# Residual input by accumulating DMA transfers, six kept sums and another split of token blocks, in a spectral filter plus MLP kernel

## The chip, the cores and the metric

The kernel runs on one core of one Trainium2 chip. The metric is the device time of one execution in microseconds (us). Eleven runs of the kernel before gave a median of 158.83 us. The engines of the core are TensorE (PE in the profile; PEld is its weight load), VectorE (DVE), ScalarE (ACT), GpSimd (POOL) and SyncE (SP, which here only issues transfers).

## What is computed

```python
def reference(A_x, A_w_r, A_w_i, B_x, B_w1, B_b1, B_w2, B_b2):
    def _A_ref(x, w_r, w_i):
        B, S, D = x.shape                       # 1, 2048, 640
        X = rfft2(x.astype(jnp.float32), axes=(-2, -1))
        X = X * (w_r + 1j * w_i)
        return irfft2(X, s=(S, D), axes=(-2, -1)).astype(jnp.bfloat16)
    def _B_ref(x, w1, b1, w2, b2):              # w1 640x1536, w2 1536x640
        h = jnp.einsum("bsd,df->bsf", x, w1) + b1
        h = _gelu(h)
        return jnp.einsum("bsf,fd->bsd", h, w2) + b2
    x = A_x
    xn = _layernorm(x, axis=-1)
    return x + _A_ref(xn, A_w_r, A_w_i) + _B_ref(xn, B_w1, B_b1, B_w2, B_b2)
```

All inputs are bf16. The output is the sum of three terms: the residual input `x`, a filter in the two-dimensional frequency domain, and an MLP with GELU. Both branches read the same normalised input.

## The kernel before

**Chunks.** The 2048 tokens are 16 chunks of 128 partitions x 640. Each chunk is loaded into `XV`, its statistics are taken (L575, L577), the reciprocal root is a power on GpSimd (L583), and the chunk is normalised (L594). For chunks 0 to 5 the transpose that the MLP needs is made on TensorE (L603); for chunks 6 to 15 by transposing transfers that SyncE issues (L614). The result is `xnT`. SyncE issues them in between the loads of the filter weights, each of which waits until the one five places earlier has landed.

**MLP, first half.** `BLOCKS` splits the chunks into seven token blocks, before: (0), (1), (2,3), (4,5), (6,7,8), (9,10,11), (12 to 15). For each block and each of 12 slices of the hidden size, five matmuls of the block's width (128, 256, 384 or 512 columns) fill a PSUM tile `hps`, and ScalarE writes `gT` from it with bias and GELU (L661). `ZONE` says which of the eight PSUM banks a tile may take, `PRIO` the rank of each kind of work.

**Spectral branch.** Both transforms are matmuls with cosine and sine tables. Forward, along tokens and features: folding adds on VectorE (L626, L630), then `gtab` matmuls into `XW`, `etab` matmuls into `Xb`, `mtab` matmuls into `Y`, for eight pairs of frequencies. The filter is L717 (products) and L722 (`Z`); small gathers `Zs` follow (L487, L488, and L485 on ScalarE). Back: `ntab` matmuls into `XV`, `getab` matmuls (one group for every two chunks) into `yo`, unfolding adds L810 (`y2`) and L815 (`yf`), and `htab` matmuls that add the last transform onto the chunk's PSUM tile.

**MLP, second half, and output.** For most chunks 24 matmuls `W`,`gT` of 320 columns and then two `htab` matmuls fill one PSUM tile `fps`. For the chunks in `STAGED` (0, 2, 4, 7, 9) the 24 matmuls are done early, while the spectral branch is in progress, and VectorE adds the bias `b2` and keeps the sum in fp32 in `xnT`, which is no longer needed by then (L796); their `htab` matmuls fill a tile of their own later. Every output chunk needs a tile `xo` of what is to be added to PSUM: SyncE loads the residual chunk into `xr` (L826), GpSimd adds it to the kept sum, or to the bias, in fp32 (L827), VectorE adds PSUM and this tile into `ost` (L840), and SyncE stores `ost` (L842). `xr` has four buffers, `xo` three and `ost` three.

**Order.** A planner (`Sched`) takes operations with an engine, a guessed duration, a priority and what they read and write, and lays down one fixed order for each engine; the time at which it ends a transfer is a guess too. A wait is put in where an operation needs another engine's or a transfer's result. The engines then run their lists in order, so an instruction that waits holds all that stands behind it on its engine. `gate` orders two operations in the plan without a wait; `after` gives a wait. Of the GpSimd adds, chunk 0's waits for the last `Z`; those of chunks 1 to 5 wait for the output add of chunk 0, and each later one for the output add five places earlier (`PACE = 5`), all by this line:

```python
port=True, reads=[xr, B_b2b] + ([B_st2[c]] if c in STAGED else []), writes=[xo], after=[z_last] + os_ops[max(c - PACE, 0):][:1])
```

The line numbers of the changed kernel lie one lower than these from the buffers' lines on, up to the output loop, where L827 becomes L826 (the bias copy) and L828 (the transfer), and L840 stays.

Of the kernel before, what the change touches and what calls it, by code (L numbers as in the profile page):

```python
# [8 lines left out]
F32 = dt.float32  # L9
# [4 lines left out]
D = 640  # L14
# [96 lines left out]
def pool_us(n):  # L111
    return 0.075 + n / 500.0


ZONE = {'hps': ((2, 8), (0, 8), (5, 8), (4, 8), (4, 8), (4, 8), (4, 8)), 'bps': (0, 4), 'cps': (0, 8), 'dps': (0, 4), 'eps': (0, 4), 'fps': (4, 8), 'fst': (4, 8), 'yps': (0, 8), 'tps': (0, 2), 'aps': (0, 6)}
PRIO = {'hps': 40.1, 'gelu': 176.7, 'pb': 71.8, 'pc': 120.9, 'filt': 194.1, 'ipc': 347.6, 'xb': 272.1, 'eps': 47.7, 'fin': 1, 'fst': 11.8}
BLOCKS = ((0, 1), (1, 2), (2, 4), (4, 6), (6, 9), (9, 12), (12, 16))
AHEAD = 2
STAGED = (0, 2, 4, 7, 9)
XRAT = 4  # L120
LAG = 5
# [63 lines left out]
class Sched:  # L185
# [10 lines left out]
    def op(self, engs, prio, emit, reads=(), writes=(), after=(), nbytes=0, gate=(), rate=360e3, bias=BIAS, port=False):  # L196
        o = Op()
        o.name = writes[0].name if writes else ""
        o.engs, o.prio, o.emit = engs, prio, emit
        o.reads, o.writes, o.after, o.gate = list(reads), list(writes), list(after), list(gate)  # L200
        o.nbytes, o.rate, o.bias, o.port = nbytes, rate, bias, port
        o.seq = len(self.ops)
        o.eng, o.done, o.inc, o.count, o.sem = None, False, False, None, None
        o.deps = [w for b in o.reads for w in b.writers] + list(after)
        for b in o.reads:
            b.readers.append(o)
        for b in o.writes:
            b.writers.append(o)
        self.ops.append(o)
        return o  # L210

    def schedule(self):
# [23 lines left out]
        while left:  # L236
# [45 lines left out]
            if o.nbytes:  # L282
                s = max(t + 1.2, dma_free)
                dma_free = s + o.nbytes / o.rate
                o.end = dma_free + (1.8 if o.seq > FAST else 0.6)
            else:
                o.end = t + dur + LAT[e]
# [105 lines left out]
def bass_parallel_sum__spectral_gfnet__dense_activation_gelu__prompt_kernel(  # L393
# [21 lines left out]
    with ExitStack() as es:  # L415
        def sb(name, shape, dtype=BF):
            return es.enter_context(nc.sbuf_tensor(name, shape, dtype))
# [33 lines left out]
        xrt = sb("xr", [128, 4, D])  # L451
        xot = sb("xo", [128, 3, D], F32)
# [17 lines left out]
        p_yo, p_y2, p_yf, p_xr, p_xo, p_os = Pool(3), Pool(2), Pool(3), Pool(4), Pool(3), Pool(3)  # L470

        def load(dst, src, buf, nbytes, after=(), reads=(), rate=330e3, eng="sp"):
            return K.op([(eng, 0.45)], 0, lambda e, _: e.dma_start(dst, src), reads=reads, writes=[buf], after=after, nbytes=nbytes, rate=rate)  # L473
# [56 lines left out]
        def load_w(dst, src, nbytes, rate):  # L530
            few.append(load(dst, src, B_w, nbytes, after=few[-DEPTH:][:1] if len(few) >= DEPTH else [], rate=rate))
# [53 lines left out]
        for c in range(16):  # L585
# [27 lines left out]
            else:  # L613
                ring_ops.append(K.op([("sp", 1.25)], 50, lambda e, _, c=c, xnv=xnv: e.dma_start(  # L614
                    xnT[:, :, 128 * c:128 * c + 128], xnv(0, [[1, D]]), transpose=True), reads=[xn], writes=[B_xnT[c]], nbytes=163840, rate=200e3))
# [33 lines left out]
        for blk, (c0, c1) in enumerate(BLOCKS):  # L649
            s0, s1 = 128 * c0, 128 * c1  # L650
            for fc in range(NFC):
                hps = Buf(f"hps{blk}_{fc}", psum, 1, ZONE["hps"][blk])
# [138 lines left out]
        def halves(v):  # L791
            return v.rearrange("p (h n) -> p h n", n=H2)
        for i, c in enumerate(STAGED):
            fps, B_st2[c] = Buf(f"fst{c}", psum, 2, ZONE["fst"]), Buf(f"sum{c}")
            st_ops += second(c, (0, 1), fps, all_hps, True)
            K.op([("dve", dve_us(D))], 86, lambda e, _, i=i, fps=fps: e.tensor_tensor(  # L796
                out=halves(xnT[:, i, 0:2 * D].bitcast(F32)), in0=ps2(fps.slot, H2), in1=halves(b2bc[:]), op=ALU.add), reads=[fps, B_b2b], writes=[B_st2[c]], after=all_hps)
        for cp in range(8):
# [20 lines left out]
            for n in range(2):  # L819
                c = 2 * cp + n  # L820
                xr, xo = Buf(f"xr{c}", p_xr), Buf(f"xo{c}", None if c in STAGED else p_xo)

                def xov(a, b, c=c, xo=xo):

                    return halves(xnT[:, STAGED.index(c), 2 * a:2 * b].bitcast(F32) if c in STAGED else xot[:, xo.slot, a:b])
                K.op([("sp", 0.35)], 0, lambda e, _, c=c, xr=xr: e.dma_start(xrt[:, xr.slot, :], xv[:, c, :]), writes=[xr], nbytes=163840, gate=pb_ops[XRAT:XRAT + 1])  # L826
                K.op([("pool", pool_us(640))], 50, lambda e, _, c=c, xr=xr, xov=xov: e.tensor_tensor(  # L827
                    out=xov(0, D), in0=halves(xrt[:, xr.slot, :]), in1=xov(0, D) if c in STAGED else halves(b2bc[:]), op=ALU.add),  # L828
                    port=True, reads=[xr, B_b2b] + ([B_st2[c]] if c in STAGED else []), writes=[xo], after=[z_last] + os_ops[max(c - PACE, 0):][:1])
                part = []  # L830
                for hs in ((0, 1),) if c < 15 else ((0,), (1,)):
                    os_, fps = Buf(f"os{c}_{hs[0]}", p_os), Buf(f"fps{c}_{hs[0]}", psum, 2, ZONE["yps" if c in STAGED else "fps"])
                    a, b = H2 * hs[0], H2 * (hs[-1] + 1)
                    if c not in STAGED:
# [6 lines left out]
                        out=halves(ost[:, os_.slot, a:b]), in0=ps2(fps.slot, H2)[:, hs[0]:hs[-1] + 1, :], in1=xov(a, b), op=ALU.add), reads=[fps, xo], writes=[os_]))  # L841
# [33 lines left out]
```

## Time and profile before

| what | value |
|---|---|
| median of 11 runs | 158.83 us (158.0 to 161.4) |
| the profiled execution | 159.16 us |
| its span in the profile | 157.4 us |
| TensorE busy | 148.1 us, 94% |
| VectorE busy | 124.8 us, 79% |
| ScalarE busy | 80.0 us, 51% |
| GpSimd busy | 31.0 us, 20% |
| granted TensorE clock | 0.998 of full speed |

The profiled execution's own time is 1.76 us above its span and 0.33 us above the median. "Busy" is the time in which an engine had an instruction in work; matmuls overlap, so two that follow each other closely count as one busy stretch. In the rows of the order of time, the first number is the start in us, the second the length, "x" the number of instructions that were merged, and the brackets hold the idle time before them with the instruction that seems to have ended it. In the table by stretch, each engine's column is its busy time, with its number of instructions. In the groups, what follows the bar is the total busy time in us and the mean of one in ns. In the list of transfers the numbers are the size in KB and the median us from issue to landing.

### The profile page before, as it was taken

How to read it: one execution, taken by the hardware profiler on the slowest of the kernel's cores; microseconds unless marked ns; L12 is line 12 of the kernel's file. 1: busy time of each engine (PE TensorE's matmuls, PEld its weight loads, DVE VectorE, ACT ScalarE, POOL GpSimd, SP SyncE). 2: the span in 40 equal slices, each digit the busy share in tenths (PEclk: the TensorE clock that was granted, in tenths of full speed). 3: DMA queues.
4: the chain of work that ended last, by engine and by line, in shares of the span. 5: the costliest groups of instructions: out<-in, count | busy, mean ns of one | idle time of the engine just before them, and what ended most of it. 6: DMA issues, size and time to landing. Idle time of an engine off the chain costs nothing.

```text
span 157.4 us, 3731 instructions
## 1 busy us (share of the span) xinstructions
PE 148.1 (94%) x1528; PEld 99.9 (63%) x1533; DVE 124.8 (79%) x263; ACT 80.0 (51%) x168; POOL 31.0 (20%) x33
## 2 busy tenths in 40 slices
PE   5799999979999999999999999899999799999993
PEld 2399799845566554445457666566776466777771
DVE  3759999979994697699498699787999999992231
ACT  3189889957777779789776456323101103100000
POOL 1201112210200000000000000300999652344200
PEclk9999999999999999999999999999999999999999
DMA  4999926979899000218513000100264433211121
GB/s 106 334 361 399 248 80 139 227 175 88 166 180 243 6 0 0 76 53 254 167 12 119 0 4 0 40 5 0 83 191 146 140 110 131 83 42 42 54 75 42
DMA packets 20648, 18.19 MB, mean 116 GB/s; under 512 B 8088, under 2 KB 19352, under 8 KB 20504
## 3 DMA queue, kind: packets, MB, share of 16 engines
q1 hardware_dynamic: 20464, 17.92, 42.4%
q8 instruction: 12, 0.20, 0.6%
q10 hardware_dynamic: 168, 0.04, 0.1%
q14 instruction: 4, 0.03, 0.1%
HBM read 13.69 MB, written 2.62 MB: 104 GB/s over the span
## 4 chain that ended last, share of the span: by engine, by line
PE 67%; DVE 12%; DMA 7%; ACT 4%; SPq 3%; POOL 3%; issue 3%; DVEq 0%; ACTq 0%
PE ps L478 66%; DMA XV<-in_A_x_dram 5%; DVE Wf L815 3%; SPq L473 3%; DMA out_dram<-ost 2%; POOL xo L827 2%; DVE ost L840 2%; ACT Xb L485 2%; DVE stats L575 1%; POOL xnT L827 1%; DVE Wf L810 1%; DVE T L717 1%; DVE xnT L796 1%; DVE Zs L488 1%; ACT Wf L485 1%
## 5 line engine op out<-in xcount | busy, mean ns | idle before, releaser
L478 PE MATMUL ps<-xnT,W 128*128 128x128 bf16 (+3 forms) x415 | 56.3, 287 | 3.0 <-ACT gT L661 1.0
L478 PE MATMUL ps<-W,gT 128*128 128x320 bf16 x384 | 56.6, 299 | 0.0
L478 PEld LDWEIGHTS ps<-W,gT 128*128 128x128 bf16 x384 | 36.7, 98 | 14.7 <-issue 0.8
L661 ACT ACTIVATE gT<-ps,b1col 128x128 bf16<-128x128 f32 (+3 forms) x84 | 39.8, 507 | 10.7 <-PE ps L478 9.7
L478 PEld LDWEIGHTS ps<-xnT,W 128*128 128x128 bf16 x420 | 34.0, 98 | 17.6 <-ACT gT L661 3.2
L827 POOL TENSOR_TENSOR xo<-xr,b2bc 128x640 f32<-128x640 bf16 x11 | 16.6, 1512 | 21.7 <-DVE ost L840 21.7
L485 ACT ACTIVATE Wf<-ps 128x640 bf16<-128x640 f32 x10 | 6.8, 703 | 25.2 <-PE ps L478 25.2
L827 POOL TENSOR_TENSOR xnT<-xr,xnT 128x640 f32<-128x640 bf16 x5 | 7.8, 1563 | 59.4 <-DVE Z L722 57.9
L840 DVE TENSOR_TENSOR ost<-ps,xo 128x640 bf16<-128x640 f32 (+1 forms) x12 | 9.1, 762 | 10.4 <-PE ps L478 10.3
L575 DVE BATCH_NORM_STATS2 stats<-XV 128x6 f32<-128x320 bf16 x32 | 14.1, 472 | 2.7 <-DMA XV<-in_A_x_dram 2.6
L815 DVE TENSOR_TENSOR Wf<-Wf 128x640 bf16<-128x640 bf16 x16 | 13.8, 893 | 0.1
L717 DVE TENSOR_TENSOR T<-Y,Wf 128x1288 bf16<-128x1288 bf16 x16 | 12.6, 828 | 0.9 <-ACT Y L485 0.4
L583 POOL TENSOR_TENSOR rstd<-ve,mhalf 128x2 f32<-128x2 f32 (+1 forms) x9 | 6.5, 720 | 33.8 <-DVE ve L582 33.8
L485 ACT ACTIVATE XV<-ps 128x640 bf16<-128x640 f32 x11 | 7.4, 703 | 5.9 <-PE ps L478 5.8
L810 DVE TENSOR_TENSOR Wf<-Wf 128x640 bf16<-128x640 bf16 x16 | 9.7, 642 | 0.8 <-ACT Wf L485 0.8
L488 DVE CAST Y<-ps 128x644 bf16<-128x644 f32 x8 | 6.6, 828 | 4.5 <-PE ps L478 4.5
L478 PE MATMUL ps<-getab,XV 128*128 128x160 bf16 (+1 forms) x128 | 8.6, 233 | 0.9 <-DVE ost L840 0.9
L485 ACT ACTIVATE Xb<-ps 128x640 bf16<-128x640 f32 x9 | 7.9, 894 | 2.7 <-PE ps L478 2.7
L478 PE MATMUL ps<-etab,XW 128*128 128x160 bf16 (+1 forms) x128 | 8.6, 233 | 0.0
L478 PEld LDWEIGHTS ps<-getab,XV 128*128 128x128 bf16 (+1 forms) x128 | 5.3, 95 | 4.3 <-DVE ost L840 1.5
L488 DVE CAST Xb<-ps 128x640 bf16<-128x640 f32 x7 | 6.2, 885 | 2.0 <-PE ps L478 2.0
L485 ACT ACTIVATE XW<-ps 128x640 bf16<-128x640 f32 x11 | 7.5, 702 | 0.6 <-PE ps L478 0.4
(51 smaller groups left out, 136.7 us busy)
## 6 DMA issues: line engine op xcount, KB each, us to landing
W<-in_B_w_dram SPq DMA_DIRECT2D x8, 480.0 KB, 4.9
xr<-in_A_x_dram SPq DMA_DIRECT2D x16, 160.0 KB, 2.3
out_dram<-ost SPq DMA_DIRECT2D x15, 160.0 KB, 1.8
XV<-in_A_x_dram SPq DMA_DIRECT2D x7, 320.0 KB, 8.1
Wf<-in_A_w_r_dram SPq DMA_DIRECT2D x7, 160.5 KB, 5.2
Wf<-in_A_w_i_dram SPq DMA_DIRECT2D x7, 160.5 KB, 3.7
gtab<-c_G SPq DMA_DIRECT2D x1, 512.0 KB, 7.4
htab<-c_H SPq DMA_DIRECT2D x1, 512.0 KB, 5.1
```

The lines of the kernel that those rows point to most:

```text
L473: return K.op([(eng, 0.45)], 0, lambda e, _: e.dma_start(dst, src), reads=reads, writes=[buf], after=after, nbytes=nbytes, rate=rate)
L478: ins = e.matmul(o_, lhsT=lw, rhs=rh, start=st, stop=sp_)
L485: return e.activation(dst(), src(), ACT.Copy, scale=scale)
L488: return e.tensor_copy(dst(), src())
L575: K.op([("dve", 0.4)], 100 - c, lambda e, _, c=c, h=h: e.bn_stats(stats[:, c, 6 * h:6 * h + 6], view(XV, c * D + H2 * h, [[1, H2]])), read ...
L583: K.op([("pool", 0.75)], 100 - c, lambda e, _, a=a, b=b: e.tensor_tensor(out=rstd[:, a:b], in0=ve[:, a:b], in1=mhalf[:, 0:b - a], op=ALU.pow),
L661: K.op([("act", act_us(s1 - s0, 1))], pr + PRIO["gelu"], lambda e, _, s0=s0, s1=s1, fc=fc, hps=hps: e.activation(gT[:, fc, s0:s1], ps(hps. ...
L717: t_ops[pair].append(K.op([("dve", 0.05 + dve_us(4 * KP, 2))], pr, lambda e, _, k=k, Y=Y, TB=TB, pair=pair: e.tensor_tensor(out=view(TT, T ...
L810: K.op([("dve", dve_us(D, 2))], pr + 2, lambda e, _, k=k, op=op, yo=yo, y2=y2: e.tensor_tensor(out=view(Wf, Y2 + y2.slot * 2 * D + (H2 - 1 ...
L815: K.op([("dve", dve_us(D, 2))], pr + 3, lambda e, _, k=k, op=op, y2=y2, yf=yf: e.tensor_tensor(out=view(Wf, YF + yf.slot * 2 * D + (D - 1) ...
L827: K.op([("pool", pool_us(640))], 50, lambda e, _, c=c, xr=xr, xov=xov: e.tensor_tensor(out=xov(0, D), in0=halves(xrt[:, xr.slot, :]), in1= ...
L840: os_ops.append(K.op([("dve", dve_us(H2 * len(hs)))], 95, lambda e, _, a=a, b=b, hs=hs, xov=xov, fps=fps, os_=os_: e.tensor_tensor(out=hal ...
```

## The change

The residual input is no longer loaded into a buffer of its own and added by GpSimd. Instead a transfer that GpSimd issues reads the bf16 chunk from memory and accumulates it into an fp32 tile in place. For the kept chunks the tile is the kept sum (which has the bias already); for the others ScalarE first copies the bias into one of five fp32 tiles `xi`. The order of who waits for whom is that of the line above: chunk 0's transfer after the last `Z`, those of chunks 1 to 5 after chunk 0's output add, the later ones after the output add five places earlier.

Kept chunks are 0, 2, 4, 6, 8, 10: six in place of five, packed one behind the other in `xnT`. The blocks are 1, 1, 2, 2, 2, 4, 4 chunks. The PSUM zones, the priorities, the lag of the spectral work behind the loads and the look-ahead of the second half take other values, and so do some of the planner's guessed durations; all of this moves instructions on their engines.

```diff
-ZONE = {'hps': ((2, 8), (0, 8), (5, 8), (4, 8), (4, 8), (4, 8), (4, 8)), 'bps': (0, 4), 'cps': (0, 8), 'dps': (0, 4), 'eps': (0, 4), 'fps': (4, 8), 'fst': (4, 8), 'yps': (0, 8), 'tps': (0, 2), 'aps': (0, 6)}
-PRIO = {'hps': 40.1, 'gelu': 176.7, 'pb': 71.8, 'pc': 120.9, 'filt': 194.1, 'ipc': 347.6, 'xb': 272.1, 'eps': 47.7, 'fin': 1, 'fst': 11.8}
-BLOCKS = ((0, 1), (1, 2), (2, 4), (4, 6), (6, 9), (9, 12), (12, 16))
-AHEAD = 2
-STAGED = (0, 2, 4, 7, 9)
+ZONE = {'hps': ((2, 8), (0, 4), (2, 8), (2, 8), (0, 4), (4, 8), (2, 8)), 'bps': (0, 4), 'cps': (0, 8), 'dps': (0, 4), 'eps': (0, 6), 'fps': (2, 8), 'fst': (0, 8), 'yps': (0, 8), 'tps': (2, 6), 'aps': (0, 8)}
+PRIO = {'hps': 41.9, 'gelu': 211.2, 'pb': 57.3, 'pc': 141.2, 'filt': 203.4, 'ipc': 358.6, 'xb': 326.2, 'eps': 56.7, 'fin': 29.1, 'fst': 17.0}
+BLOCKS = ((0, 1), (1, 2), (2, 4), (4, 6), (6, 8), (8, 12), (12, 16))
+AHEAD = 3
+STAGED = (0, 2, 4, 6, 8, 10)
 XRAT = 4
-LAG = 5
+LAG = 4
...
-                o.end = dma_free + (1.8 if o.seq > FAST else 0.6)
+                o.end = dma_free + (1.8 if o.seq > FAST else 0.6) + o.lat
...
-        xrt = sb("xr", [128, 4, D])
-        xot = sb("xo", [128, 3, D], F32)
+        xot = sb("xo", [128, 5, D], F32)
...
-                xr, xo = Buf(f"xr{c}", p_xr), Buf(f"xo{c}", None if c in STAGED else p_xo)
-
-                def xov(a, b, c=c, xo=xo):
-
-                    return halves(xnT[:, STAGED.index(c), 2 * a:2 * b].bitcast(F32) if c in STAGED else xot[:, xo.slot, a:b])
-                K.op([("sp", 0.35)], 0, lambda e, _, c=c, xr=xr: e.dma_start(xrt[:, xr.slot, :], xv[:, c, :]), writes=[xr], nbytes=163840, gate=pb_ops[XRAT:XRAT + 1])
-                K.op([("pool", pool_us(640))], 50, lambda e, _, c=c, xr=xr, xov=xov: e.tensor_tensor(
-                    out=xov(0, D), in0=halves(xrt[:, xr.slot, :]), in1=xov(0, D) if c in STAGED else halves(b2bc[:]), op=ALU.add),
-                    port=True, reads=[xr, B_b2b] + ([B_st2[c]] if c in STAGED else []), writes=[xo], after=[z_last] + os_ops[max(c - PACE, 0):][:1])
+                xi, xo = B_st2.get(c) or Buf(f"xi{c}", p_xo), Buf(f"xo{c}")
+
+                def xov(a, b, c=c, xi=xi):
+
+                    return view(xnT, 2 * D * STAGED.index(c) + 2 * a, [[1, 2 * b - 2 * a]]).bitcast(F32) if c in STAGED else xot[:, xi.slot, a:b]
+                if c not in STAGED:
+                    K.op([("act", act_us(640))], 30, lambda e, _, xov=xov: e.activation(xov(0, D), b2bc[:], ACT.Copy), reads=[B_b2b], writes=[xi],
+                         gate=[z_last] + os_ops[max(c - PACE, 0):][:1])
+                K.op([("pool", 1.2)], 50, lambda e, _, c=c, xov=xov: e.dma_start(xov(0, D), xv[:, c, :], accum_op=ALU.add), reads=[xi], writes=[xo],
+                     after=[z_last] + os_ops[max(c - PACE, 0):][:1], nbytes=163840, lat=1.0)
...
-                        out=halves(ost[:, os_.slot, a:b]), in0=ps2(fps.slot, H2)[:, hs[0]:hs[-1] + 1, :], in1=xov(a, b), op=ALU.add), reads=[fps, xo], writes=[os_]))
+                        out=halves(ost[:, os_.slot, a:b]), in0=ps2(fps.slot, H2)[:, hs[0]:hs[-1] + 1, :], in1=halves(xov(a, b)), op=ALU.add), reads=[fps, xi, xo], writes=[os_]))
```

## The prediction

> **What bounds the kernel now.** I read the busy time by stage first, then the order of time on TensorE, because TensorE is busy for 94% of the span and the few places where it is not are all that a change around it can win.
>
> ```profile
> core 0: us, PE busy (x) PEld busy (x) DVE busy (x) ACT busy (x) POOL busy (x), PEclk, DMA share, GB/s
> 16.50:32.50 16.00, 14.96 (x151) 13.27 (x152) 16.00 (x57) 13.71 (x30) 3.11 (x4) 1.00 0.70 163
> ...
> 100.70:127.60 26.90, 25.72 (x260) 17.76 (x260) 24.42 (x31) 5.53 (x8) 15.35 (x10) 1.00 0.33 99
> 127.60:154.80 27.20, 27.12 (x216) 19.05 (x216) 16.83 (x28) 2.00 (x3) 7.33 (x5) 1.00 0.21 71
> 154.80:157.40 2.60, 0.00 (x0) 0.00 (x0) 0.46 (x1) 0.00 (x0) 0.00 (x0) 0.89 0.11 32
> ```
>
> From 127.6 on TensorE never stops; nothing is to be won there, nor in the 2.6 us after its last matmul, which the change leaves alone. TensorE idles 1.04 us of the second stretch and 1.18 us between 100.7 and 127.6, and 0.70 just before that. The order of time names the three places:
>
> ```profile
> 32.45 0.97 PE L478 MATMUL ps<-xnT,W 128*128 128x384 bf16 x5 [1.04 <-ACT gT L661]
> ...
> 100.77 0.62 PE L478 MATMUL ps<-ntab,Z 64*128 64x128 bf16 x16 [0.70 <-DVE Zs L488]
> ...
> 124.17 1.08 PE L478 MATMUL ps<-getab,XV 128*128 128x160 bf16 x16 [0.93 <-DVE ost L840]
> ```
>
> **The wait of 1.04.** It stands before the first 384-wide matmul, the block of chunks 6 to 8. The GELU that is named ended at 31.92, so it is not what ended the wait at 32.45. SyncE's order of time has the other candidate:
>
> ```profile
> 28.65 2.61 SPq L614 DMA_TRANSPOSE xnT<-Z  x2
> ...
> 33.92 2.60 SPq L614 DMA_TRANSPOSE xnT<-Z  x2
> ```
> ```profile
> DMA to landing us min/median/max: 2.7/3.6/5.2
> ```
>
> Chunk 8's transposing transfer is issued at 28.65 and lands, by the median, at 32.25. So TensorE waited for chunk 8. In the new split the block after chunks 4 and 5 takes 6 and 7 alone, which were issued at 23.34: the wait goes. What is late next? The block of 8 to 11 needs chunk 11. TensorE reaches it after 180 matmuls of 256 columns (0.1095 each: 35 took 3.82), two transposes and four groups of gtab work (0.28 and 0.56): 16.46 + 19.7 + 0.56 + 2.24 = 39.0. Chunk 11 is issued at 35.2 now (second of the pair at 33.92); SyncE's new order has ten filter loads before that pair where it had eleven (0.6 us less), so 34.6, landing at 38.2, or 39.8 by the longest landing. VectorE is the other limit: it was busy from 16.5 to 47.05 but for 1.01 us at 33.0, where it waited for TensorE behind this same wait, so it can follow by 1.0. I take -1.0; bounds -1.3 (TensorE also meets 0.3 us less block work before the first etab group) and 0. Matmul work itself is unchanged: 60 matmuls for each of seven blocks and the same columns.
>
> **The wait of 0.70.** Its cause stands in the window 99 to 101:
>
> ```profile
> 99.10 1.44 POOL L827 TENSOR_TENSOR xnT<-xr,xnT 128x640 f32<-128x640 bf16 x1 [57.86 <-DVE Z L722]
> 99.19 1.43 DVE L488 COPY Zs<-Z 128x128 bf16<-128x128 bf16 x1
> ```
>
> Such a copy takes 0.22 at 69.41; here it ends with GpSimd's add. Without it, TensorE would be free at 99.89 (24 matmuls from 96.63 at 0.136), 0.88 earlier. In the change GpSimd issues chunk 0's accumulating transfer at that very moment. The trace has no such issue: at least 0.34 (SyncE's issue of the same load, at 100.56), at most 1.6 (the add it replaces). I take 1.0, between the two, as neither is near. Held for a whole issue of 1.0 in place of 1.44, the copy gives back 0.44; not held, 0.88. I take -0.5, near the held one, since a held copy is what the row shows; bounds -0.88 and 0.
>
> **VectorE in the output stage.**
>
> ```profile
> L815 DVE TENSOR_TENSOR Wf<-Wf 128x640 bf16<-128x640 bf16 x16 | 13.8, 893 | 0.1
> ...
> L810 DVE TENSOR_TENSOR Wf<-Wf 128x640 bf16<-128x640 bf16 x16 | 9.7, 642 | 0.8 <-ACT Wf L485 0.8
> ```
>
> Single ones beside an idle GpSimd take 0.47 (133.51, 138.25); the longest is 1.7. Sixteen GpSimd adds of 1.5 us leave: 16 x (0.893 - 0.47) + 16 x (0.642 - 0.47) = 9.5 us of VectorE. One more kept sum adds 0.82 (L796). Ten ScalarE copies of the bias at some 0.70 add 7.0 to an engine that is busy 7.5 of 54 us; three of them wait for an output add, with only a later yo copy behind each, and by my walk none of these is late. SyncE loses 16 loads (0.34 each) that waited for GpSimd ahead of output stores. After this a pair of chunks costs VectorE 0.82 + 4 x 0.45 + 2 x 0.74 = 4.1 us, and TensorE 24 x 0.136 + 2 x 0.28 + 0.91 = 4.74, so TensorE sets the pace. Let T be the start of the last ntab group. Walking the new order: chunk 0's matmuls end at T+6.0, its output add at T+7.5 (now T+9.4), the sixth kept sum's first matmul starts at T+7.6, yf1 makes TensorE wait 0.4 at T+9.4; I find no other wait. Of 1.18 idle, 0.5 stays: -0.7; bounds -1.1 and 0.
>
> **The accumulating transfer itself.** Chunks 1 to 5 are all held until chunk 0's output add, as before, and then issued one after another. The add that used the tile at once after 1.57 us now waits for a landing.
>
> ```profile
> xr<-in_A_x_dram SPq DMA_DIRECT2D x16, 160.0 KB, 2.3
> ...
> XV<-in_A_x_dram SPq DMA_DIRECT2D x7, 320.0 KB, 8.1
> ```
>
> Landing L from issue: at least 2.3, the same bytes without the fp32 tile; at most 8.1, the slowest plain load, twice as large and in the crowded first 20 us. The fp32 tile, read and written, is 640 KB more; at the best slice's 399 GB/s that is 1.6, so I take 2.3 + 1.6 = 4, nearer the lower row because DMA is 33% busy there. Needs: chunk 4's tile, fourth in the row, at T+15.8 (after chunk 1's output): 7.5 + 3 x 1.0 + 4 = 14.5, good until L = 5.3. Chunks 6, 8 and 10 are issued after the output adds of 1, 3 and 5 and needed 5.5 later. So it hides, and costs nothing until L = 5.5; above it some 4 x (L - 5.5), since VectorE is in order and the next yf and the next PSUM slot stand behind each late add. A gain from this part is excluded: an output add can only wait for it.
>
> The Trainium skill has a rule against this edit. SBUF — State Buffer, section "Who interferes with whom", says that VectorE and GpSimd lock one port pair for a whole instruction, and that descriptors of a GpSimd-issued DMA starve while VectorE copies in a two-port mode, whereas two-input tensor operations collide only with GpSimd's reads. The row for the collision is the 1.43 us copy above; by the rule the copy is held for the whole issue (-0.44 in place of -0.5), the 9.5 us of VectorE are still freed, as L810 and L815 have two inputs and an issue reads no tile, and an issue that meets such a copy starts late. DMA: Bandwidth & Descriptors, section "Anatomy of one DMA", puts such a transfer at 2.0 us plus bytes over 436 GB/s: 2.4 us as an estimate for 160 KB; no run here shows either yet, and by it L would have 3 us to spare.
>
> **Sum.** -1.0 - 0.5 - 0.7 = -2.2: span 157.4 to 155.2, the profiled run 159.16 to 156.96; the median of the runs lies 0.33 below that run, so 156.6.
>
> **Rivals.** (1) The transfer lands late. Place: the output adds of chunks 4, 6, 8, 10. It decides from L = 6.05, where 4 x 0.55 eats 2.2; at 6.5 the time is 158.8 - 2.2 + 4.0 = 160.6, at 8.1 it is 167. For it: no row shows an accumulate into fp32, and several run at once. Against it: 2.3 us for the same load with a third of the DMA time used. (2) Issuing holds VectorE as the adds did: -0.5 and -0.7 go, 157.8. For it, the 1.43 us copy; against it, an issue need not read the tile. (3) Chunk 11 lands late (5.2): TensorE waits 0.8 at 39, 157.4 to 157.6. For it, a margin of 0.8; against it, one load fewer ahead of it on SyncE.
>
> **How the numbers follow.** Forecast 0.45 (own range 155.4 to 157.6), late landing 0.33, port 0.12, chunk 11 0.10. 0.3%, what a measurement here can tell from no change, is 0.5 us: 158.35 to 159.31. Of the late landings 0.05 fall inside it and 0.28 above; the two small rivals stay below but for 0.04 that falls inside. Faster 0.63, same 0.09, slower 0.28. Range: down to 155.2 (all gains at their bounds, -3.3, and the spread of the runs), up to 161.2, a landing of 6.65, beyond which I leave 0.12.
>
> **What would show it.** No wait at the first block of 6 and 7 and none over 0.3 at the first 512-wide matmul; the Zs copy below 1.2 us and the last ntab group within 0.3 of the matmuls before it; L810 and L815 means at 0.5; output adds that wait for TensorE and not for the transfer; landing below 5.5. Wrong if output adds wait for the xo or xnT transfer and TensorE for those adds.

## The result and the profile after

The changed kernel takes 156.32 us (median of 12 runs, 155.32 to 157.04) against 158.83 before. The ratio of the mean times, without two slow runs of the kernel before, is 0.9846, with a 95% interval of 0.9826 to 0.9866. A later measurement gave 156.01 against 158.71, ratio 0.9822 (0.9784 to 0.9859). The first profiled execution of the changed kernel took 156.94, with a span of 155.0 us, at the upper end of its twelve (153.2 to 155.0); a second one, taken later, took 155.97 with a span of 153.9.

First the order of time on TensorE in the first profile after, at the ends of the stretches that the prediction speaks of:

```profile
47.27 1.08 PE L477 MATMUL ps<-etab,XW 128*128 128x160 bf16 x16
...
98.06 0.62 PE L477 MATMUL ps<-ntab,Z 64*128 64x128 bf16 x16
...
124.18 0.45 PE L477 MATMUL ps<-Wf,htab 128*128 128x320 bf16 x2 [0.78 <-DVE Wf L814]
124.91 3.43 PE L477 MATMUL ps<-W,gT 128*128 128x320 bf16 x24 [0.29 <-DVE ost L840]
```

The two waits that stood before 49.26 and at 100.77 are gone; the last `ntab` group carries no bracket any more. In the output stage TensorE still waits 1.07 us, as long as before, but for other things. VectorE's order of time shows which:

```profile
112.02 0.82 DVE L840 TENSOR_TENSOR ost<-ps,xnT 128x640 bf16<-128x640 f32 x1 [1.76 <-DMA xnT<-in_A_x_dram]
...
114.38 0.82 DVE L840 TENSOR_TENSOR ost<-ps,xnT 128x640 bf16<-128x640 f32 x1 [0.32 <-DMA xnT<-in_A_x_dram]
...
121.57 0.82 DVE L840 TENSOR_TENSOR ost<-ps,xnT 128x640 bf16<-128x640 f32 x1 [2.12 <-DMA xnT<-in_A_x_dram]
```

These are the output adds of the kept chunks 2, 4 and 6, and each waits for its accumulating transfer. Behind the third stand two pairs of unfolding adds (122.31 to 124.12), and `htab` at 124.18 waits for them. The groups show what VectorE won, and what GpSimd and ScalarE do now:

```profile
L809 DVE TENSOR_TENSOR Wf<-Wf 128x640 bf16<-128x640 bf16 x16 | 7.2, 485 | 1.4 <-ACT Wf L484 1.3
L814 DVE TENSOR_TENSOR Wf<-Wf 128x640 bf16<-128x640 bf16 x16 | 7.2, 489 | 0.3
...
L826 ACT ACTIVATE xo<-b2bc 128x640 f32<-128x640 bf16 x10 | 7.0, 735 | 3.5 <-DVE ost L840 3.3
```

The unfolding adds took 23.5 us in sum and take 14.4. GpSimd's order of time shows the transfers of chunks 1 to 5 leaving in one burst as soon as chunk 0's output add is done:

```profile
106.19 0.88 POOL L828 DMA_DIRECT2D xo<-in_A_x_dram  x1 [7.77 <-DVE ost L840]
106.74 1.23 POOL L828 DMA_DIRECT2D xnT<-in_A_x_dram  x1
107.29 1.58 POOL L828 DMA_DIRECT2D xo<-in_A_x_dram  x1
107.84 1.94 POOL L828 DMA_DIRECT2D xnT<-in_A_x_dram  x1
108.39 2.29 POOL L828 DMA_DIRECT2D xo<-in_A_x_dram  x1
...
114.36 0.88 POOL L828 DMA_DIRECT2D xnT<-in_A_x_dram  x1 [0.34 <-DVE ost L840]
```

One issue alone takes 0.88 us. From issue to landing the five needed 3.8, 5.3, 5.9, 6.5 and 7.2 us, and chunk 6's (114.36) 7.1. The queues and one stretch show how busy the DMA engines are (queue: packets, MB, share of the 16 DMA engines' span; stretch: span, busy time of the five engines, granted clock, DMA share, GB/s):

```profile
q0 software_dynamic: 2304, 5.24, 15.3%
```
```profile
110.00:114.00 4.00, 4.00 (x32) 2.85 (x30) 1.85 (x3) 0.00 (x0) 1.53 (x2) 1.00 1.11 255
```

15.3% of 155.0 us over 16 transfers is 1.48 us of packet time on all 16 DMA engines for each. Packet times overlap (a share of 1.11 is more than the whole), so 1.48 is not how long one transfer keeps the others out. That is better read from the ends. The five issues start 0.55 apart but end (start plus length) 0.90 apart, at 107.07 to 110.68, about the 0.88 of a single one: by these rows GpSimd works them off one after another. Their landings follow 1.1 to 1.3 us apart behind the second. So of the 3.4 us by which the fifth takes longer than the first, 1.4 pass on GpSimd before its issue has ended, and 2.0 after it, while the DMA share is about 1.1.

The last column of the table below is what follows the last matmul; the others are distances read from the order of time on TensorE in one profiled execution each. The second profile of the kernel before is one of the experiments, as are the rows below it.

| kernel | first 256-wide matmul to first `etab` | to last `ntab` | to end of last matmul | rest of span |
|---|---|---|---|---|
| before, first profile | 32.80 | 51.51 | 53.96 | 2.67 |
| before, second profile | 32.68 | 51.51 | 53.95 | 2.64 |
| after, first profile | 31.27 | 50.79 | 53.84 | 3.10 |
| after, second profile | 31.28 | 50.79 | 52.94 | 3.03 |
| blocks alone | 30.70 | 52.80 | 55.54 | 2.59 |
| GpSimd adds back | 31.28 | 51.56 | 53.86 | 2.64 |
| transfers alone | 32.39 | 50.75 | 58.04 | 3.05 |
| early transfers | 31.27 | 50.80 | 53.77 | 3.05 |
| early transfers, fourth slot (two profiles) | 31.27 | 50.79 | 52.53, 52.54 | 3.09, 3.07 |
| fourth slot alone | 31.88 | 50.79 | 52.65 | 3.03 |
| conversion without adding | 31.27 | 50.79 | 52.42 | 3.08 |
| add behind `Zs` | 32.17 | 50.75 | 53.96 | 2.66 |

### The profile page after: what moved, and what is told of

Same layout as the page of the kernel before. It is cut to its first block, busy times and chain, and to the rows that moved or that the text cites. A ratio compares the mean times of both kernels' runs of the same rounds, so it can differ in the third digit from the quotient of the medians.

```text
span 155.0 us, 3728 instructions
## 1 busy us (share of the span) xinstructions
PE 147.3 (95%) x1525; PEld 100.7 (65%) x1533; DVE 116.6 (75%) x265; ACT 86.7 (56%) x177; POOL 21.0 (14%) x33
## 3 DMA queue, kind: packets, MB, share of 16 engines
q0 software_dynamic: 2304, 5.24, 15.3%
## 4 chain that ended last, share of the span: by engine, by line
PE 80%; DMA 8%; DVE 5%; SPq 3%; issue 1%; ACT 1%; DVEq 0%
PE ps L477 79%; DMA XV<-in_A_x_dram 5%; DMA xnT<-in_A_x_dram 3%; SPq L472 3%; DVE ost L840 1%; ACT Xb L484 1%; DVE stats L574 1%; DVE Wf L809 1%; DVE Wf L487 1%; DVE T L593 0%; PE ps L602 0%; DVE Wf L814 0%; DVE xnT L487 0%; DVE mv L576 0%; DVEq L376 0%
## 5 line engine op out<-in xcount | busy, mean ns | idle before, releaser
L477 PE MATMUL ps<-xnT,W 128*128 128x256 bf16 (+2 forms) x412 | 55.3, 286 | 1.8 <-issue 0.6
L477 PEld LDWEIGHTS ps<-W,gT 128*128 128x128 bf16 x384 | 36.6, 98 | 15.5 <-DVE ost L840 0.9
L660 ACT ACTIVATE gT<-ps,b1col 128x256 bf16<-128x256 f32 (+2 forms) x84 | 40.0, 506 | 8.0 <-PE ps L477 5.5
L477 PEld LDWEIGHTS ps<-xnT,W 128*128 128x128 bf16 x420 | 34.7, 98 | 14.5 <-issue 1.3
L840 DVE TENSOR_TENSOR ost<-ps,xo 128x640 bf16<-128x640 f32 (+1 forms) x11 | 8.4, 763 | 12.3 <-PE ps L477 12.3
L828 POOL DMA_DIRECT2D xnT<-in_A_x_dram x6 | 6.7, 1137 | 61.6 <-DVE Zs L486 57.0
L828 POOL DMA_DIRECT2D xo<-in_A_x_dram x10 | 10.4, 1087 | 19.9 <-DVE ost L840 17.2
L826 ACT ACTIVATE xo<-b2bc 128x640 f32<-128x640 bf16 x10 | 7.0, 735 | 3.5 <-DVE ost L840 3.3
L809 DVE TENSOR_TENSOR Wf<-Wf 128x640 bf16<-128x640 bf16 x16 | 7.2, 485 | 1.4 <-ACT Wf L484 1.3
L840 DVE TENSOR_TENSOR ost<-ps,xnT 128x640 bf16<-128x640 f32 x6 | 4.9, 820 | 4.2 <-DMA xnT<-in_A_x_dram 4.2
L477 PEld LDWEIGHTS ps<-etab,XW 128*128 128x128 bf16 (+1 forms) x128 | 5.5, 95 | 3.8 <-DVE Y L487 0.7
L477 PE MATMUL ps<-Wf,htab 128*128 128x320 bf16 x32 | 7.1, 299 | 0.8 <-DVE Wf L814 0.8
```

The source lines that it names most:

```text
L477: ins = e.matmul(o_, lhsT=lw, rhs=rh, start=st, stop=sp_)
L660: K.op([("act", act_us(s1 - s0, 1))], pr + PRIO["gelu"], lambda e, _, s0=s0, s1=s1, fc=fc, hps=hps: e.activation(gT[:, fc, s0:s1], ps(hps. ...
L809: K.op([("dve", dve_us(D, 2))], pr + 2, lambda e, _, k=k, op=op, yo=yo, y2=y2: e.tensor_tensor(out=view(Wf, Y2 + y2.slot * 2 * D + (H2 - 1 ...
L826: K.op([("act", act_us(640))], 30, lambda e, _, xov=xov: e.activation(xov(0, D), b2bc[:], ACT.Copy), reads=[B_b2b], writes=[xi], gate=[z_l ...
L828: K.op([("pool", 1.2)], 50, lambda e, _, c=c, xov=xov: e.dma_start(xov(0, D), xv[:, c, :], accum_op=ALU.add), reads=[xi], writes=[xo], aft ...
L840: os_ops.append(K.op([("dve", dve_us(H2 * len(hs)))], 95, lambda e, _, a=a, b=b, hs=hs, xov=xov, fps=fps, os_=os_: e.tensor_tensor(out=hal ...
```

## The experiments

### The parts of the change one by one

**Blocks alone**: the kernel before with the new split.

```diff
-BLOCKS = ((0, 1), (1, 2), (2, 4), (4, 6), (6, 9), (9, 12), (12, 16))
+BLOCKS = ((0, 1), (1, 2), (2, 4), (4, 6), (6, 8), (8, 12), (12, 16))
```

> The kernel before with one value changed: blocks of 2 and 4 chunks (6,7 and 8 to 11) in place of 3 and 3. Theory: the 1.04 us wait of TensorE before the first matmul of the block of 6 to 8 was for chunk 8's transposing transfer, so it goes and the first etab group starts 1.0 to 1.5 us earlier after the first 256-wide matmul (now 32.8 us); time 157.4 to 158.0. Rival, the retuned priorities, lag and PSUM zones made that gain: 158.5 or more, with a wait of 0.7 or more left at that place or a new one of that size at the first 512-wide matmul.

Measured: 158.88 us, ratio 1.0035 (1.0004 to 1.0066). The wait of 1.04 is gone and the first stretch is 2.1 us shorter, so the place was right. But the gain is lost twice behind it, 1.3 us in the second stretch and 1.6 in the third. Part of this is work that the planner put off: 296 `W`,`gT` matmuls stand behind the last `ntab` where before had 292, and TensorE is busy there for 53.9 us in place of 52.8. The rest is waiting. The order of time in the second stretch shows how:

```profile
51.59 1.57 DVE L717 TENSOR_TENSOR T<-Y,Wf 128x1288 bf16<-128x1288 bf16 x2 [1.49 <-DMA Wf<-in_A_w_i_dram]
...
54.00 0.74 PE L478 MATMUL ps<-Xb,mtab 64*64 64x322 bf16 x16 [0.96 <-DVE Xb L488]
```

TensorE now comes to the filter before the last filter weights have landed: VectorE waits 1.49 for them, and TensorE 0.96 behind it. In the output stage TensorE waits 1.35 for VectorE, where before it waited 1.11. The split wins only together with an order that has something else for TensorE to do there. The other values of the change (priorities, zones, lag, look-ahead, a sixth kept sum) give such an order, as the next run shows; which of them matters was not tried.

**GpSimd adds back**: the changed kernel with the loads into `xr` (four buffers) and the adds of before (three `xo`), all else as changed.

```diff
-                    K.op([("act", act_us(640))], 30, lambda e, _, xov=xov: e.activation(xov(0, D), b2bc[:], ACT.Copy), reads=[B_b2b], writes=[xi],
...
-                K.op([("pool", 1.2)], 50, lambda e, _, c=c, xov=xov: e.dma_start(xov(0, D), xv[:, c, :], accum_op=ALU.add), reads=[xi], writes=[xo],
...
+                K.op([("sp", 0.35)], 0, lambda e, _, c=c, xr=xr: e.dma_start(xrt[:, xr.slot, :], xv[:, c, :]), writes=[xr], nbytes=163840, gate=pb_ops[XRAT:XRAT + 1])
+                K.op([("pool", pool_us(640))], 50, lambda e, _, c=c, xr=xr, xov=xov: e.tensor_tensor(
...
```

> The changed kernel with GpSimd's residual loads and adds back in place of the accumulating transfers and the bias copies; blocks, six kept sums and every other value stay. Theory: first 256-wide matmul to first etab group stays near 31.3 us; the wait for the Zs copy before the last ntab group returns (0.7, the copy 1.2 us or longer); VectorE's L809 and L814 take 0.6 to 0.9 us on the mean again, and TensorE's time from the last ntab group to its end is 53.8 to 54.6 us. Time 157.0 to 157.8. Rival, the transfers carry most of the gain: 158.2 or more.

Measured: 157.15 us, ratio 0.9905 (0.9874 to 0.9935); against the changed kernel's 156.32, from another set of runs, the transfers are worth some 0.8 (0.9 by the two ratios). Of the gain over before, the order and the blocks carry the larger part. The order of time of this kernel has the collision of before again, with the same 1.43 and 0.70:

```profile
96.83 1.44 POOL L827 TENSOR_TENSOR xnT<-xr,xnT 128x640 f32<-128x640 bf16 x1 [56.81 <-DVE Z L722]
96.93 1.43 DVE L488 COPY Zs<-Z 128x128 bf16<-128x128 bf16 x1
...
98.50 0.63 PE L478 MATMUL ps<-ntab,Z 64*128 64x128 bf16 x16 [0.70 <-DVE Zs L488]
```

**Transfers alone**: the kernel before with the accumulating transfers, the bias copies and five tiles, but its own blocks, kept chunks, zones and priorities.

```diff
-        xrt = sb("xr", [128, 4, D])
-        xot = sb("xo", [128, 3, D], F32)
+        xot = sb("xo", [128, 5, D], F32)
...
-                K.op([("pool", pool_us(640))], 50, lambda e, _, c=c, xr=xr, xov=xov: e.tensor_tensor(
...
+                    K.op([("act", act_us(640))], 30, lambda e, _, xov=xov: e.activation(xov(0, D), b2bc[:], ACT.Copy), reads=[B_b2b], writes=[xi],
...
+                K.op([("pool", 1.2)], 50, lambda e, _, c=c, xov=xov: e.dma_start(xov(0, D), xv[:, c, :], accum_op=ALU.add), reads=[xi], writes=[xo],
...
```

> The kernel before with the accumulating transfers and the bias copies (five tiles) alone; old blocks, five kept sums, old values. Theory: the 1.04 us wait for chunk 8 stays, the 0.7 us wait for the Zs copy goes, the output stage gains nothing: 157.8 to 158.6. Rival, the transfers carry most of the gain: 157.0 or less. Rival, the transfers only cost in an order that was not made for them: 159.3 or more, with output adds that wait for them for over 5 us in all.

Measured: 161.81 us, ratio 1.0215 (1.0173 to 1.0258): slower than before by more than the whole change gains. In front of the last `ntab` group it gains 0.76, as the change does; the output stage then takes 58.04 in place of 53.96. The waits of this kernel (us in all, times, longest) name the chain:

```profile
POOL xo L828 <- ACT xo L826: 15.6, 3, 9.4
...
ACT xo L826 <- DVE ost L840: 6.7, 4, 2.8
DVE ost L840 <- DMA xnT<-in_A_x_dram: 4.9, 3, 3.3
...
PE ps L477 <- DVE ost L840: 3.5, 3, 1.8
```

Output adds wait 4.9 for transfers, as in the changed kernel (4.2), but in this order TensorE has nothing to put in their place and waits 3.5 for them, and 1.4 more for a ScalarE copy and an unfolding add. ScalarE's copies stand in line too, since its bias copies wait 6.7 for output adds. Waits for late landings of about the same size go with 4 us lost in one order and about 1 in the other; that they are the cause of all 4 is not shown.

**Add behind `Zs`**: the kernel before, where chunk 0's GpSimd add also waits for the last gathers; TensorE, VectorE and ScalarE keep their order.

```diff
+            zs_ops = list(ZS.writers)
...
-                    port=True, reads=[xr, B_b2b] + ([B_st2[c]] if c in STAGED else []), writes=[xo], after=[z_last] + os_ops[max(c - PACE, 0):][:1])
+                    port=True, reads=[xr, B_b2b] + ([B_st2[c]] if c in STAGED else []), writes=[xo], after=[z_last] + zs_ops + os_ops[max(c - PACE, 0):][:1])
```

> The kernel before, with GpSimd's add of chunk 0 released by the last gathers into Zs instead of by the last Z; order on TensorE, VectorE and ScalarE as before, the add starts about 0.3 us later. Theory: VectorE's last copy into Zs takes 0.22 us in place of 1.43, TensorE's wait of 0.70 before the last filter group goes, and nothing behind it loses what was won: time 0.5 to 0.9 below before (157.9 to 158.3 where before is 158.8). Rival (the slack is taken up behind it, in the output stage, by the add that now starts later or by VectorE): wait gone, but the time within 0.3 of before.

Measured: 158.12 against 158.98 us, ratio 0.9939 (0.9906 to 0.9973). The copy is short, the group comes without a wait, and the output stage is as long as before (53.96):

```profile
98.08 0.22 DVE L488 COPY Zs<-Z 128x128 bf16<-128x128 bf16 x1
98.72 1.41 POOL L828 TENSOR_TENSOR xnT<-xr,xnT 128x640 f32<-128x640 bf16 x1 [58.60 <-ACT Zs L485]
98.88 0.62 PE L478 MATMUL ps<-ntab,Z 64*128 64x128 bf16 x16
```

That isolates the second term of the sum: 51.51 to 50.75, 0.76 us, from one more wait on GpSimd. The kernel before could have had it without any transfer.

### Where the gain of the output stage stays

**Early transfers**: the changed kernel, with the kept chunks' transfers released by the last `Z` and their own kept sum, and those of chunks 1, 3 and 5 no longer held by chunk 0's output add.

```diff
-                     after=[z_last] + os_ops[max(c - PACE, 0):][:1], nbytes=163840, lat=1.0)
+                     after=[z_last] + os_ops[c - PACE:][:1] if c > PACE and c not in STAGED else [z_last], nbytes=163840, lat=1.0)
```

> The changed kernel with the transfers of the kept chunks issued as soon as the last Z and their own sum are there, and those of chunks 1, 3 and 5 no longer held for the first output add. Theory: the landing of 5 to 7 us is queueing, since five to eight transfers of some 1.5 us of all DMA engines each are issued within 10 us; spread out, they land in time, the output adds' waits for transfers (4.2 us in all) fall below 1 and TensorE's waits of 0.78 and 0.29 at 124 go: 155.0 to 155.8. Rival, a landing of 5 us and more is the transfer's own: the waits stay above 2 us and the time within 0.4 of 156.3.

Measured: 156.56 us, ratio 0.9868 (0.9829 to 0.9907), no better than the changed kernel. No output add waits for a transfer any more, so it was the transfers that held them. That queueing alone makes a transfer late is not shown by this run: the median landing stays at 4.1 us (`xo`) and 5.7 (`xnT`), only the issue comes earlier. And TensorE waits as long as before, elsewhere:

```profile
118.89 0.82 DVE L840 TENSOR_TENSOR ost<-ps,xo 128x640 bf16<-128x640 f32 x1 [2.10 <-PE ps L477]
...
119.77 0.45 PE L477 MATMUL ps<-W,gT 128*128 128x320 bf16 x2 [1.06 <-DVE ost L840]
```

The bracket at 118.89 names TensorE, but the two `htab` matmuls that this add reads ended at 117.52. The add also needs a slot of `ost`, and there are three: it waits for the store that used the slot last. For the store issued at 112.1 the trace of this kernel has

```profile
DMA to landing us min/median/max: 6.7/6.7/6.7
```

and 112.1 + 6.7 is 118.8. A store that meets no transfers landed in 1.8. So the transfers delay the stores, and the stores hold VectorE. That was a new theory, tested with a fourth slot.

**Early transfers with a fourth slot.** Every engine's order is that of the run above.

```diff
-        ost = sb("ost", [128, 3, D])
+        ost = sb("ost", [128, 4, D])
...
-        p_yo, p_y2, p_yf, p_xo, p_os = Pool(3), Pool(2), Pool(3), Pool(5), Pool(3)
+        p_yo, p_y2, p_yf, p_xo, p_os = Pool(3), Pool(2), Pool(3), Pool(5), Pool(4)
```

> The kernel of the run with early transfers (kept chunks' transfers released by the last Z and their own sum), with a fourth slot in the result tile ost, 640 more bf16 values in each partition; the order of the instructions on every engine is that of that run. Theory: the output add at 118.89 there did not wait for TensorE but for the store that last used its slot (issued at 112.1, landed 6.7 us later, at 118.8, because the stores share the DMA engines with the accumulating transfers; a store alone landed in 1.8). A fourth slot takes that wait away: the add starts at about 117.6, TensorE's wait of 1.06 before its first 24 matmuls of the next chunk falls below 0.2, last filter group to last matmul 52.8 to 53.1 in place of 53.77, and the time is 155.5 to 155.8 (ratio to before about 0.981). Rival (the wait belongs to TensorE's late matmuls and to VectorE's order): it stays at about 1 us and the time at 156.4 to 156.7.

Measured: 156.08 us, ratio 0.9837 (0.9793 to 0.9882), and the order of time

```profile
118.16 0.82 DVE L840 TENSOR_TENSOR ost<-ps,xo 128x640 bf16<-128x640 f32 x1 [0.78 <-PE ps L477]
...
119.14 2.06 PE L477 MATMUL ps<-W,gT 128*128 128x320 bf16 x14
```

The add now starts as soon as its matmuls (117.69 to 118.12) are done, and TensorE has no wait left in the stage: 52.53 us from the last `ntab` to the last matmul. The store was the cause of that wait. The time lies above the 155.5 to 155.8 that was expected, and its interval overlaps that of the run before.

**Fourth slot alone**: the same two lines in the changed kernel, and nothing else.

> The changed kernel with a fourth slot in the result tile ost and nothing else; same order on every engine. Theory: its waits of 1.76 and 2.12 us before output adds of kept chunks are for accumulating transfers (the last one issued at 114.36, landed 7.1 us later, at 121.5), so stores that land late hold nobody there: waits stay, time 156.1 to 156.5. Rival (the stores alone hold the adds): waits of the output adds fall below 1 us in sum and the time is 155.5 to 155.8.

Measured: 156.59 us, ratio 0.9885 (0.9838 to 0.9931). Waits of the kept chunks' output adds: 1.66, 0.24, and 0.92 whose cause the trace does not name, 2.8 in all against 4.2. The waits lie between the two theories; TensorE did not wait in this execution, and yet the time is not lower. One profile of each kernel was not enough here, which is why both kernels were profiled again.

**The changed kernel and the version with early transfers and a fourth slot, once more, on one chip.**

> The changed kernel once more, unaltered: a second profile of it, and its time on the same chip as the version with early transfers and a fourth result slot. Its first profile was the longest of its twelve executions (span 155.0, the others 153.2 to 155.0), so its waits may not be the usual ones. Theory: the late transfers and stores are part of every execution; last filter group to last matmul is 53.2 to 53.9 again, with output adds waiting 3 to 5 us for transfers, and TensorE 0.5 to 1.1 us for VectorE. Rival: the profiled execution was an unlucky one; the stretch is 52.5 to 52.9, TensorE waits for nothing in it, and the kernel needs no earlier transfers.

> The version with early transfers and a fourth result slot once more, for its time beside the changed kernel's on one chip. Theory: last filter group to last matmul 52.5 to 52.6 again with no wait of TensorE in it, time 0.3 to 1.0 below the changed kernel's. Rival: the changed kernel's slack takes the same waits up in most executions; the two times agree within 0.3.

Measured: 156.01 (ratio 0.9822, 0.9784 to 0.9859) and 156.03 us (0.9833, 0.9790 to 0.9875): no difference. The second profile of the changed kernel has the same waits of VectorE, but the last is shorter:

```profile
112.00 0.82 DVE L840 TENSOR_TENSOR ost<-ps,xnT 128x640 bf16<-128x640 f32 x1 [1.87 <-DMA xnT<-in_A_x_dram]
...
114.50 0.82 DVE L840 TENSOR_TENSOR ost<-ps,xnT 128x640 bf16<-128x640 f32 x1 [0.56 <-DMA xnT<-in_A_x_dram]
120.53 0.82 DVE L840 TENSOR_TENSOR ost<-ps,xnT 128x640 bf16<-128x640 f32 x1 [1.08 <-DMA xnT<-in_A_x_dram]
```
```profile
123.88 3.43 PE L477 MATMUL ps<-W,gT 128*128 128x320 bf16 x24 [0.22 <-DVE ost L840]
```

Chunk 6's transfer, issued at 114.2, landed in 6.2 us in place of 7.1, and TensorE waited 0.22 in place of 1.07. So each theory was half right: the late transfers are there in both profiled executions, but what they cost TensorE hangs on how late the last of them is, 0.2 in an execution near the median, 1.1 in one of the longest. The earlier transfers and the fourth slot remove a wait of that size and win nothing that the runs can tell.

**Conversion without adding**: the changed kernel, whose transfers overwrite the tile. The bias and the kept sums are left out of the output.

```diff
-                K.op([("pool", 1.2)], 50, lambda e, _, c=c, xov=xov: e.dma_start(xov(0, D), xv[:, c, :], accum_op=ALU.add), reads=[xi], writes=[xo],
+                K.op([("pool", 1.2)], 50, lambda e, _, c=c, xov=xov: e.dma_start(xov(0, D), xv[:, c, :]), reads=[xi], writes=[xo],
```

> The changed kernel with transfers that convert to fp32 and overwrite the tile instead of adding to it (so the bias and the kept sums are left out of the output); same order on every engine. It measures what the accumulation itself costs beside the conversion. Theory: adding makes the engines read the fp32 tile as well, so without it a transfer takes 0.7 to 1.1 us of the 16 DMA engines in place of 1.48 and lands in 3.0 to 4.5 in place of 5.1; the waits of output adds for transfers fall from 4.2 to below 1.5 us; time 155.5 to 156.1. Rival (conversion through the software queue sets the price, 128 rows of 2560 bytes written whatever is done with them): 1.4 to 1.5 us, landing 5, waits 4, time as the changed kernel's, 156.1 to 156.5.

Measured: 155.79 us, ratio 0.9820 (0.9781 to 0.9859). The page of this kernel, queue and landings:

```profile
q0 software_dynamic: 2304, 5.24, 12.3%
...
xo<-in_A_x_dram POOLq DMA_DIRECT2D x10, 320.0 KB, 3.1
...
xnT<-in_A_x_dram POOLq DMA_DIRECT2D x6, 320.0 KB, 3.2
```

12.3% of 153.3 us over 16 is 1.18 us of packet time on all 16 DMA engines for a transfer in place of 1.48, a little above the range expected; the median landing is 3.1 to 3.2 in place of 4.6 and 5.3, and no output add waits for a transfer. The shortest landing is 2.9 in place of 3.7, so the adding itself costs some 0.8 us, 0.34 of it in the issue (0.54 in place of 0.88). The rest of the difference in the medians goes with the crowding: in this kernel the burst of five lands in 3.0 to 4.2 us, one every 0.83. The time is 0.2 to 0.5 below the changed kernel's, within the intervals.

**The kernel before, once more**, for a second profile.

> The kernel before, unaltered, for a second profile of it: which of the waits that the prediction counted are there in every execution. Its first profile took 159.16 against a median of 158.83. Theory: the waits are the kernel's own; about 1.0 us before the first 384-wide matmul, 0.7 before the last filter group, 1.2 us in the output stage. Rival: the first of them varies, since it hangs on the start of a transposing transfer against the matmuls that run ahead (0.41 and 0.64 were seen in two versions with the same order there); then it is 0.4 to 0.7, and first 256-wide matmul to first group of the forward transform is 32.1 to 32.5 in place of 32.80.

Measured: one execution of 158.09 us. The waits were 0.92, 0.70 and 0.93 + 0.18; the first stretch was 32.68. The wait before the 384-wide block varies, since it is the difference of two starts, but its end stands at a fixed distance from a transfer:

```profile
31.39 0.97 PE L478 MATMUL ps<-xnT,W 128*128 128x384 bf16 x5 [0.92 <-ACT gT L661]
```
```profile
27.65 2.59 SPq L614 DMA_TRANSPOSE xnT<-Z  x2
```

31.39 is 3.74 after that issue; in the first profile it was 3.80 (28.65 and 32.45). Two other versions keep the order of before up to here, the add behind `Zs` (issue at 27.61) and transfers alone (28.02):

```profile
31.32 0.97 PE L478 MATMUL ps<-xnT,W 128*128 128x384 bf16 x5 [0.41 <-ACT gT L661]
```
```profile
31.75 0.97 PE L477 MATMUL ps<-xnT,W 128*128 128x384 bf16 x5 [0.64 <-ACT gT L660]
```

That is 3.71 and 3.73. In all four the block starts 3.7 to 3.8 us after chunk 8's transposing transfer is issued, and in the first profile that transfer landed 3.7 us after its issue, at 32.35. So the rival was right in part: the wait runs from 0.41 to 1.04.

## Why the prediction held, point by point

**The wait before the 384-wide block, -1.0.** Measured -1.5 and -1.4: 32.80 and 32.68 became 31.27 and 31.28 in two profiles each. The cause was read rightly (chunk 8's transfer, not the GELU in the bracket). But the term holds two parts. Without its wait, the first stretch of the order of before is 31.75 to 31.76 in all four executions (32.80 - 1.04, 32.68 - 0.92, 32.39 - 0.64, 32.17 - 0.41), so 0.41 to 1.04 was the wait, and some 0.5 comes from the rest of the stretch. The prediction had this second part only in its bound of -1.3, as 0.3 us less block work. Nor is the stretch always 31.27: in the run with the fourth slot alone it was 31.88, with a wait of 0.40 for a fold of VectorE, so that from one execution to another the gain is 0.3 to 1.5. Chunk 11, the rival, did not come late: no wait at the first 512-wide matmul in either profile.

**The wait before the last `ntab`, -0.5.** Measured -0.72, and -0.76 alone. The step that failed is "I take -0.5, near the held one": the copy was not held, and the whole wait went. Here is chunk 0's issue in the first profile after:

```profile
97.25 0.22 DVE L487 COPY Zs<-Z 128x128 bf16<-128x128 bf16 x1
97.39 1.04 POOL L828 DMA_DIRECT2D xnT<-in_A_x_dram  x1 [57.03 <-DVE Zs L486]
```

Before, GpSimd's add started 0.09 us ahead of the copy; the issue starts 0.14 after the copy's start, so the two meet for 0.08 us. The prediction had the issue at the very moment of the add. Whether an issue that starts first would hold a copy stays unmeasured.

**VectorE in the output stage, -0.7.** The relief was as worked out: 9.1 us off the unfolding adds (9.5 predicted), one more kept sum, bias copies of 0.735 (0.70 predicted) that TensorE never waits for. TensorE's stage became 0.1 us shorter in the first profile and 1.0 in the second. The prediction's walk found one wait of 0.4, for an unfolding add, and no other; that one is not there, and the waits that are there come from transfers. Without late landings (conversion without adding; early transfers with a fourth slot) the stage takes 52.4 to 52.5, against 53.96 before and 53.86 with GpSimd's adds in the new order. So the new order by itself is worth 0.1 here and the relief 1.3 to 1.4, and the late landings give 0.4 to 1.4 of it back.

**The accumulating transfer, 0.** This is the step whose mechanism was wrong. L was taken as one number, 4, and the same for each; its median came out at 5.1, just under the 5.5 at which it was to cost something, but L depends on what else is under way: 3.7 with little else, up to 7.2 in the burst of five. The prediction saw that chunks 1 to 5 are issued one after another and priced the issues about rightly (1.0 us each, 0.90 measured), but not the queue behind them: the landings of the burst come 1.1 to 1.3 us apart, and the fifth needs 2.0 more than the first after its issue has ended. Its walk also named the wrong chunk. It took chunk 4's tile as the first to be late; it was chunk 2's, whose add VectorE was free for at 110.26, 3.5 us after the issue at 106.74. That is less than the 4 that was predicted, and less than the shortest landing of 3.7. "Output adds that wait for TensorE and not for the transfer" was wrong. So was the rival's price of 4 x (L - 5.5): the late ones were chunks 2, 4 and 6, and of those only chunk 6's add had something behind it that TensorE soon needed. Chunks 8 and 10 were issued when the burst was over (5.3 and 3.7 us). Something of the rival's size does occur in another order: 4 us with the transfers alone.

**Holding by the issue** (the second rival) is excluded for two-input adds. While the five transfers were being issued, VectorE ran, in the first profile after,

```profile
107.61 0.88 DVE L809 TENSOR_TENSOR Wf<-Wf 128x640 bf16<-128x640 bf16 x2
108.53 0.90 DVE L814 TENSOR_TENSOR Wf<-Wf 128x640 bf16<-128x640 bf16 x2
```

0.44 to 0.45 for one, no more than the 0.47 beside an idle GpSimd. That agrees with what the Trainium skill says in SBUF — State Buffer, section "Who interferes with whom": a VectorE instruction with two SBUF inputs collides with a GpSimd instruction that reads SBUF, and not with one that only writes it; the residual tile, which the add of before read, an issue does not read. The skill's other figure does not fit: 2.0 us plus bytes over 436 GB/s (DMA: Bandwidth & Descriptors, section "Anatomy of one DMA") gives an estimate of 2.4 us for 160 KB, while the shortest accumulating transfer here took 3.7, and the shortest that only converts 2.9. The measurement decides.

**The sum.** -2.2 was predicted and -2.5 measured, but not because all terms were right: that the number came out so near is in part luck, since the terms that were too small and the costs left at nothing nearly cancel. By the second profiles the three stretches give -1.40 - 0.72 - 1.01 = -3.1. Two things that the prediction left at nothing take 0.6 back. What follows the last matmul grew from 2.65 to 3.05, in every kernel with transfers from GpSimd and in none without. And the time outside the span grew from 1.80 (median over the runs of the kernel before) to 2.03; with GpSimd adds back it is 1.78. The time before the first 256-wide matmul is left out of this sum: it varies from 15.5 to 16.5 us between executions. The prediction said that the change leaves the end alone. The trace names no instruction for it: the last store is issued 0.56 us after the last matmul and lands in 1.6 in both kernels, so the longer end lies behind that landing. Its cause was not tried.

## What to carry to other kernels

Price a transfer that takes over an add twice: the issue on its own engine, and the time between two landings when they follow each other, against the rate at which such transfers are released; a release line that lets five go at once is a queue. And look for the add with the least time between its transfer's issue and its own turn: here it was the second of the five. Then ask who shares the DMA engines: here the output stores landed up to 6.7 us after their issue and kept a slot of the result tile, and the bracket of the waiting add named TensorE. And before a cause is read from a wait of 0.2 to 1 us, look at a second profile: between two executions of one kernel, the same wait was 1.07 and 0.22.

## What the runs showed of the hardware that was not expected

- An accumulating transfer from bf16 to an fp32 tile of 128 x 640 takes 0.88 us to issue on GpSimd and lands 3.7 us after the start of its issue at the least; in a burst of five the issues end 0.90 apart and the landings follow 1.1 to 1.3 apart from the second on. Converting without adding takes 0.54 to issue and 2.9 to land, 0.83 apart in the burst. Packet time on all 16 DMA engines is 1.48 and 1.18 us. Both are counted as 5.24 MB for 16, that is, by the bytes of the fp32 side.
- A store of 160 KB that landed in 1.8 us when no such transfer was under way took up to 6.7 beside them.
- The end of the program after the last matmul took 0.4 us longer in all kernels with such transfers, also where they did not add.
